# Attention with nine consecutive tokens per partition, and key-value products as row-tiled pairs of K=64

## The chip, the cores and the metric

The kernel runs on one core of one Trainium2 chip. The metric is device time in microseconds (us), the median of several executions; executions of one kernel agree within about 2%. One profiled execution per kernel gives the trace that the readings below come from; its span is about 2 us shorter than the device time. PE is TensorE's matrix unit, PEld its weight loads, DVE is VectorE, ACT is ScalarE, POOL is GpSimd, SP the engine that issues most transfers. K is the number of rows over which a matmul sums, the first number of forms such as `128*128` and `64*128` in the profile; 128 is the largest in these traces, and a matmul with K=128 is called a full-array matmul here. A warming matmul has no useful result; it is there to keep TensorE's clock up (e11, with more of them in the head than e6, ran the same last 36 K=64 matmuls of the head in 1.31 us instead of 2.10).

## The reference

Linear attention, then a two-layer network with a gated unit, in fp32:

```python
# q, k, v: [8 batches, 8 heads, 576 tokens, 64]
q_s = exp(q - max) / sum over the 64 dims;   k_s = exp(k - max) / sum over the 576 tokens
kv  = einsum('bhsd,bhse->bhde', k_s, v)      # 64x64 per head
x   = einsum('bhsd,bhde->bhse', q_s, kv)     # -> [4608 tokens, 512]
h   = x @ w_in                               # 512 -> 2048
out = (h / (1 + exp(-beta * h))) @ w_out     # 2048 -> 512
```

## The kernel before

Everything of the big products is bf16. The 4,608 tokens are cut in nine slabs of 512: slab `t` (0 to 7) holds the first 512 tokens of batch `t`, slab 8 the remaining 64 tokens of all eight batches. Each slab takes 64 matmuls of 128x128 weights and 512 columns for the first layer ("pass 1", `PS<-XT,WIN`) and 64 for the second ("pass 2", `PS<-WOUT,GT`). The attention of a later batch is woven into the slabs: `spread(steps, lo, hi)` places its small matmuls at positions lo to hi of the 128.

A main load puts 4 consecutive tokens of each head on each of 128 partitions (rows of 1024 bytes); the other 64 tokens of a batch come by "remainder" loads, rows of 256 bytes, 64 partitions per batch:

```python
def src(th, b, h0, nh):
    return bass.AP(th, (b * H + h0) * S * D, [[4 * D, 128], [S * D, nh], [1, 4 * D]])
def load_rem(name, th, buf, b, hs=(0, 1)):
    for h in hs:
        a = bass.AP(th, (b + h) * H * S * D + SM * D, [[D, SR], [S * D, H], [1, D]])
        ...dma_start(buf[64 * h:64 * h + 64, :, :], a)
# key-value product: per head pair, 4 matmuls of K=128 and one for the remainder
#   (K=128 too: the other batch's half of V is zero), 20 per batch
mm(PS[bk][:, 256*n:256*n + 129], l, r_[:, 0:129], j == 0, j == 4, ...)
def attn(b):                                   # batches 3 to 7, in slabs 2 to 6
    s = spread(kv_steps(b, (0, 1)) + kv_steps(b, (2, 3)), 8, 36)
    ... # output products at 84..108, remainder output at 104..120
```

The softmax here doesn't subtract the row's maximum and nothing guards it: scores larger than these inputs give would overflow.

## Time and profile before

| | before |
|---|---|
| device time | 295.69 us, median of 3 |
| span of the profiled run | 293.8 us |
| slab 0 starts (end of the head) | 17.11 us |
| slab 0 (with the attention of batch 1 after it) | 36.58 us |
| slabs 3 to 6 | 29.62 to 29.86 us each |
| slab 7, no attention in it | 27.63 us |

The starts of slabs are the starts of their first `PS<-XT,WIN` matmul in the timeline.

The page of the profile: busy time of each engine with its share of the span, and the number of instructions; and the chain of waits that ended last, by engine:

```profile
span 293.8 us, 3723 instructions
PE 281.1 (96%) x1470; PEld 132.5 (45%) x1499; DVE 114.3 (39%) x226; ACT 164.3 (56%) x248; POOL 43.2 (15%) x69
...
PE 75%; DMA 12%; SPq 8%; POOL 2%; issue 1%; DVE 1%; ACT 0%
```

TensorE is the bound. A piece of slab 4 in the timeline (start, length, engine, line, operation, what is written from what, number; the lengths overlap because matmuls are pipelined, so read the differences of the starts):

```profile
147.42 0.22 PE L345 MATMUL PS<-VB,EK 128*128 128x129 bf16 x1
147.48 0.38 PE L345 MATMUL PS<-XT,WIN 128*128 128x512 bf16 x1
147.69 0.22 PE L345 MATMUL PS<-VB,EK 128*128 128x129 bf16 x1
147.75 0.59 PE L345 MATMUL PS<-XT,WIN 128*128 128x512 bf16 x2
148.18 0.22 PE L345 MATMUL PS<-VB,EK 128*128 128x129 bf16 x1
```

A 512-column matmul holds the array for 0.2155 us (147.48 to 147.69, and 0.43 for two), a key-value matmul for 0.055 us (147.42 to 147.48). Its weight load is hidden: the one of the matmul at 147.42 is at 147.21 and takes 0.10 us, under the 512-column matmul before it, which holds the array from 147.20 to 147.42. Both are of the form `128*128`: weight loads and matmuls on the same rows do overlap here.

The stages in windows (window, its length, then busy time and number of PE, PEld, DVE, ACT, POOL, the clock granted to TensorE, DMA share, GB/s); the stages are the head, slabs 0, 2, 4 and 7:

```profile
0.00:17.11 17.11, 13.46 (x86) 6.06 (x88) 8.97 (x27) 10.81 (x19) 11.79 (x27) 0.90 0.98 235
17.11:53.69 36.58, 33.34 (x190) 15.42 (x193) 17.29 (x40) 21.84 (x34) 6.20 (x9) 1.00 1.15 284
84.86:115.58 30.72, 29.87 (x158) 14.20 (x160) 14.79 (x26) 18.92 (x28) 6.80 (x10) 1.00 1.03 297
145.21:175.06 29.85, 29.69 (x158) 14.28 (x160) 14.80 (x26) 18.34 (x27) 3.50 (x4) 1.00 0.26 69
234.54:262.17 27.63, 27.47 (x127) 12.51 (x128) 2.77 (x4) 11.00 (x16) 0.00 (x0) 1.00 0.09 39
```

The transfers are busy through slab 2 (last two columns) and then stop mattering. How long some of the loads take from issue to landing (KB each, median us):

```profile
QF<-in_q_dram SPq DMA_DIRECT2D x6, 1024.0 KB, 8.0
VF<-in_v_dram SPq DMA_DIRECT2D x6, 1024.0 KB, 11.8
```

And of the waits of PE, the lines of the transposed Q (`QT`), whose wait falls in slab 2, and of the normalized Q (`EQ`) in the head and slab 0 (us in total, times, longest):

```profile
PE PS L343 <- POOL EQ L308: 1.6, 3, 0.9
PE PS L343 <- DVE EQ L308: 1.2, 1, 1.2
PE PS L345 <- DMA QT<-EQ: 0.7, 1, 0.7
```

### The profile page before, as it was taken

Reading aid. Unit: us, or ns where it says so; the run is one execution under the profiler, and the core shown is the slowest. Engines: PE = TensorE matmul, PEld = TensorE weight load, DVE = VectorE, ACT = ScalarE, POOL = GpSimd, SP = SyncE. Lnnn points to the kernel's source line nnn. Section 1 sums busy time; section 2 is a strip of 40 time slices with the busy share of each in tenths; the row PEclk is TensorE's granted clock in tenths of the full one; section 3 lists DMA queues with packets and bytes.
Section 4 is the critical chain, followed back from the end, with each engine's and each line's share of the span. In section 5 each row is a group of like instructions: output and inputs, shape, how many; then the busy total and the mean of one; then the engine's idle time right before and its main releaser. Section 6 shows DMA issues by size and latency. Waiting matters only on the chain.

```text
span 293.8 us, 3723 instructions
## 1 busy us (share of the span) xinstructions
PE 281.1 (96%) x1470; PEld 132.5 (45%) x1499; DVE 114.3 (39%) x226; ACT 164.3 (56%) x248; POOL 43.2 (15%) x69
## 2 busy tenths in 40 slices
PE   6999998899999989999999999999999999999994
PEld 2444444344545434544454445444544444444441
DVE  5430686313688044704391447133913400110011
ACT  4878444879677870688068907790670077017500
POOL 6640015024605200600040000000000000000000
PEclk9799999999999999999999999999999999999999
DMA  7999999999999999904970006000810030002022
GB/s 200 286 189 249 382 315 245 336 269 347 294 302 275 354 244 318 247 0 152 315 215 20 1 1 212 4 0 0 203 31 0 2 143 0 2 36 107 0 74 71
DMA packets 58290, 47.32 MB, mean 161 GB/s; under 512 B 26000, under 2 KB 54688, under 8 KB 57248
## 3 DMA queue, kind: packets, MB, share of 16 engines
q1 hardware_dynamic: 53728, 44.45, 53.3%
q0 software_dynamic: 4224, 2.10, 5.3%
q10 hardware_dynamic: 320, 0.52, 0.5%
q8 instruction: 12, 0.20, 0.3%
q14 instruction: 6, 0.05, 0.1%
HBM read 36.71 MB, written 9.44 MB: 157 GB/s over the span
## 4 chain that ended last, share of the span: by engine, by line
PE 75%; DMA 12%; SPq 8%; POOL 2%; issue 1%; DVE 1%; ACT 0%
PE PS L345 74%; SPq L251 5%; DMA VF<-in_v_dram 3%; DMA WIN<-in_moe_w_in_dram 3%; DMA QT<-EQ 3%; SPq L258 2%; DMA WST<-in_moe_w_out_dram 2%; DMA KF<-in_k_dram 2%; POOL WIN L555 1%; DVE WOUT L542 1%; SPq L629 0%; PE PS L343 0%; ACT GT L618 0%; DVE O2S L623 0%; POOL VB L323 0%
## 5 line engine op out<-in xcount | busy, mean ns | idle before, releaser
L618 ACT ACTIVATE GT<-PS,BETA 128x512 bf16<-128x512 f32 x144 | 98.4, 687 | 89.6 <-PE PS L345 89.6
L345 PE MATMUL PS<-WOUT,GT 128*128 128x512 bf16 x561 | 131.7, 379 | 0.6
L345 PE MATMUL PS<-XT,WIN 128*128 128x512 bf16 x564 | 130.9, 379 | 1.2 <-ACT XT L417 0.7
L345 PEld LDWEIGHTS PS<-WOUT,GT 128*128 128x128 bf16 x576 | 54.5, 98 | 62.2
L345 PEld LDWEIGHTS PS<-XT,WIN 128*128 128x128 bf16 x576 | 53.5, 98 | 62.3 <-ACT XT L417 1.0
L623 DVE COPY O2S<-PS 128x512 f32<-128x512 f32 x34 | 23.3, 687 | 112.6 <-PE PS L345 112.5
L345 PE MATMUL PS<-VB,EK 128*128 128x129 bf16 (+2 forms) x160 | 25.1, 209 | 1.6 <-POOL VB L323 1.4
L323 POOL CAST VB<-VF 128x512 bf16<-128x512 f32 x28 | 18.5, 662 | 35.7 <-PE PS L345 26.0
L280 ACT ACTIVATE EQ<-QF 128x512 bf16<-128x512 f32 x32 | 18.1, 619 | 9.7 <-DMA QF<-in_q_dram 9.5
L417 DVE CAST XT<-PS 128x512 bf16<-128x512 f32 x27 | 18.5, 689 | 12.0 <-PE PS L345 12.0
L306 DVE TENSOR_REDUCE QS<-EQ 128x8 f32<-128x512 bf16 (+1 forms) x22 | 20.1, 912 | 7.5 <-ACT EQ L280 7.5
L280 ACT ACTIVATE EK<-KF 128x512 bf16<-128x512 f32 x32 | 17.9, 616 | 0.9 <-DMA KF<-in_k_dram 0.7
L345 PEld LDWEIGHTS PS<-VB,EK 128*128 128x128 bf16 x160 | 13.0, 98 | 11.2 <-POOL VB L323 2.5
L308 DVE TENSOR_TENSOR EQ<-EQ,QI 128x1024 bf16<-128x1024 bf16 (+1 forms) x14 | 15.2, 1084 | 0.5
L345 PE MATMUL PS<-QT,KVD 128*128 128x512 bf16 x32 | 12.0, 381 | 1.2 <-DMA QT<-EQ 0.7
L308 POOL TENSOR_TENSOR EQ<-EQ,QI 128x512 bf16<-128x512 bf16 x8 | 8.3, 1042 | 33.0 <-DVE QI L307 32.7
L380 DVE SCALAR_TENSOR_TENSOR KVD<-PS,RC,MASK 128x128 bf16<-128x128 f32 x32 | 11.1, 350 | 3.6 <-PE PS L345 2.5
L331 POOL CAST VR<-VRF 64x512 bf16<-64x512 f32 x8 | 6.2, 776 | 40.4 <-DMA VRF<-in_v_dram 40.0
L345 PE MATMUL PS<-WARM 128*128 128x512 bf16 x28 | 10.8, 509 | 1.3 <-DVE WARM L219 1.2
L542 DVE TENSOR_SCALAR WOUT<-WST,RB 128x512 bf16<-128x512 f32 x12 | 5.0, 480 | 14.4 <-DMA WST<-in_moe_w_out_dram 14.4
L343 PE MATMUL PS<-IDB,EQ 128*128 128x128 bf16 x48 | 6.1, 228 | 2.7 <-POOL EQ L308 1.6
L345 PE MATMUL PS<-VR,EKR 128*128 128x129 bf16 (+2 forms) x40 | 8.2, 208 | 0.1
(55 smaller groups left out, 93.1 us busy)
## 6 DMA issues: line engine op xcount, KB each, us to landing
out_dram<-O2S SPq DMA_DIRECT2D x8, 1024.0 KB, 4.5
QF<-in_q_dram SPq DMA_DIRECT2D x6, 1024.0 KB, 8.0
KF<-in_k_dram SPq DMA_DIRECT2D x6, 1024.0 KB, 9.7
VF<-in_v_dram SPq DMA_DIRECT2D x6, 1024.0 KB, 11.8
WST<-in_moe_w_out_dram SPq DMA_DIRECT2D x3, 1024.0 KB, 6.7
QF<-in_q_dram SPq DMA_DIRECT2D x8, 256.0 KB, 6.0
KF<-in_k_dram SPq DMA_DIRECT2D x8, 256.0 KB, 6.5
VF<-in_v_dram SPq DMA_DIRECT2D x8, 256.0 KB, 6.6
```

Source lines behind the costliest of these rows:

```text
L251: add(SP, lambda e, c=c: e.dma_start(dst(bufs[i], c * n, n), src(th, b, c * n, n)), w=[(name, i, hp) for hp in range(c * n // 2, (c + 1) * ...
L280: add(ACTE, lambda e, o=o, a=a: e.activation(o, a, ACT.Exp), r=[(name + "f", i, hp)], w=[("e" + name, i, hp)])
L306: add(DVE, lambda e: e.tensor_reduce(s_, a, AX.X, ALU.add), r=ks, w=[("qs", i, hp0)])
L308: add(eng, lambda e: e.tensor_tensor(a, a, vb, ALU.mult), r=ks + [("qi", i, hp0)], w=ks)
L323: add(eng, lambda e: (e.copy if eng == ACTE else e.tensor_copy)(o, a), r=[("vf", i, hp), ("vone", i)], w=[("vb", i, hp)])
L331: add(POOL, lambda e, o=o, a=a: e.tensor_copy(o, a), r=[("vrf", h), ("vrone", pi, h), ("vr0", pi, h)], w=[("vr", pi, h)])
L345: add(PE, lambda e: e.matmul(o, l, r_, start=start, stop=stop), r=r, w=w, bank=[bk])
L380: add(DVE, lambda e: e.scalar_tensor_tensor(KVD[i][:, hp, :], PS[bk][:, c:c + 128], RC[i][:, hp:hp + 1], MASK[:, :], ALU.mult, ALU.mult), ...
L417: add(eng, lambda e: (e.copy if eng == ACTE else e.tensor_copy)(XT[i][:, hp, :], PS[bk][:, :]), r=[("ps", bk)], w=[("xt", i, hp)], bank=[bk])
L542: add(DVE, lambda e, f=f: e.tensor_scalar(WOUT[:, f, :], STAGE[c][:, f % 4, :], RB[:, f:f + 1], None, ALU.mult), r=SKEY[c] + ["rb"], w=[(" ...
L618: add(ACTE, lambda e: e.activation(GT[:, f, :], PS[bk][:, :], ACT.Silu, scale=BETA[:, f:f + 1]), r=[("ps", bk), "beta"], w=[("gt", f)], ba ...
L623: add(eng, lambda e: (e.copy if eng == ACTE else e.tensor_copy)(O2S[t % 2][:, u, :], PS[bk][:, :]), r=[("ps", bk)], w=[("o2", t % 2, u)], ...
```

## The change

Its intent: put all 576 tokens of a head in one layout, 9 consecutive tokens (2304 bytes) on each of 64 partitions, heads 0 to 3 on partitions 0 to 63 and heads 4 to 7 on 64 to 127. The remainder loads, their exponentials, casts, zero fills and sums go. The two halves belong to different heads, so a key-value product contracts over 64 partitions: a pair of K=64 matmuls, one on the upper and one on the lower rows of the array, into two PSUM banks. The stores of the result are cut into two halves of 64 partitions as well (not shown).

```diff
+G = 64
+NJ = S // G                                   # 9
-        def load_main(name, th, bufs, b, split=1): ...     (128 partitions x 1024 B)
-        def load_rem(name, th, buf, b, hs=(0, 1)): ...     (64 partitions x 256 B)
+        def load_one(name, th, bufs, b, split=1):
+            for c in range(split):
+                for hh in range(2):
+                    a = bass.AP(th, (b * H + 4 * hh + c * n) * S * D,
+                                [[NJ * D, G], [S * D, n], [1, NJ * D]])
+                    o = bass.AP(bufs[i], hh * G * 4 * NJ * D + c * n * NJ * D,
+                                [[4 * NJ * D, G], [NJ * D, n], [1, NJ * D]])
+                    add(SP, lambda e, o=o, a=a: e.dma_start(o, a), ...)
...
+        def kv_mm(b, lp, j, bks, c0, c1, n0, n1, first, last, vals):
+            for hh in range(2):
+                p = slice(hh * G, hh * G + G)
+                mm(PS[bks[hh]][:, c0:c1], EK[i][p, lp, j, :], VB[i][p, lp, j, n0:n1], first, last, ...)
...
         def attn(b):
-            s = spread(kv_steps(b, (0, 1)) + kv_steps(b, (2, 3)), 8, 36)
+            s = spread(kv_steps(b), 8, 36)       # 2 x 9 pairs
...                                             (fewer warming matmuls in the head; steps of 1152 columns)
```

## The prediction

> **What bounds the kernel now.** TensorE. The page gives PE 96% busy, every other engine 56% or less; the chain of waits is 75% PE. The big matmuls (128x512, 1,152 of them) follow each other every 0.2155 us in the timeline, so 248 us of the 293.8 us span is their streaming at granted clock 1.00. From 53.7 us to the end (236 us) I count 1,024 x 0.2155 + 120 key-value matmuls x 0.055 + 24 output matmuls x 0.215 + small ones = 235 us: no idle to win. Non-streaming time is in two places: the head (first slab starts at 17.1 us) and the stretch between slabs 0 and 1 (47.0 to 53.7 us), where PE waits for the V loads and their casts.
>
> **What the change does.**
> 1. Remainder loads go (256 B rows), and Q/K/V rows become 2304 B. Packet times in the trace (18 ns per 256 B, 48 per 1024 B, 84 per 2048 B) give about 9.0 instead of 10.4 us of DMA for batch 0. After slab 1 the DMA is not on the path: worth nothing there.
> 2. Exponentials, casts, sums become fewer and larger (1152 columns; 0.63 us per 512 now, so an estimated 1.3 us). Less work for ScalarE and VectorE, off the path in steady state; in the head and before slab 1 the last cast and the coarser pipeline cost about 1 us each, eating gain 1. [...]
> 3. Per batch, 20 key-value matmuls of K=128 become 18 pairs of K=64. In the timeline of slab 4 one of the 20 costs 0.055 us, weight load hidden behind its neighbours: 1.1 us per batch. If pairs run side by side and loads stay hidden, 18 x 0.06: nothing gained, nothing lost. Run serially: +0.9 us per batch, +5 in all.
> 4. But each pair stands alone between full-array matmuls (18 steps spread over 28 slots): about 99 changes to the half-array and back in batches 2 to 7. [...] No row pair is in this trace; the nearest is the 16-row beta transpose: the matmul before it stops streaming at 12.84 us, its weight load starts only at 12.93 (not pulled ahead, nothing awaited), and the next full matmul starts at 13.10. That round trip is 0.26 us, though it is also an f32 operation. At about 0.27 us per visit instead of 0.06, 99 visits add an estimated 21 us, all on the critical path.
>
> **Prediction.** I hold step 4 slightly likelier than not. Without it: 295 to 300 us. With it: 308 to 330. My middle, 308 us, lies between; range 293 to 325. Faster by over 2%: 3%; within 2%: 40%; slower: 57%.
>
> **What would show it.** In the timeline of slabs 2 to 6, first half: gaps of 0.1 us or more in PE streaming before and after each pair, weight loads of pairs not overlapping the preceding matmul; slabs with attention several us longer than slabs 7 and 8 (27.7 us). If step 4 is wrong, a pair's two matmuls start some ns apart and the next 512-column matmul follows within 0.06 (parallel) or 0.11 us (serial). Windows of 0 to 20 and 45 to 56 us show steps 1 and 2: start of slab 0 at 16 to 19 us, of slab 1 within 2 us of before.
>
> **What would make it wrong.** [...] the head gains more from longer DMA rows than I allow; [...]

The 21 us of step 4 rest on the 0.26 us of the beta transpose. Added up from 295.69 us: about 296 us without step 4 (1.4 us won in step 1, twice about 1 us lost in step 2) and about 317 us with it. The middle of 308 us was not this sum but lies between the two.

## The result, and the profile after

The changed kernel is correct and takes 333.91 us (median of 4, 332.17 to 334.72) against 296.35 us for the kernel before in the same rounds: ratio 1.126, 95% interval 1.120 to 1.132. A ratio here is the mean time of one kernel's fast runs over that of the other's of the same rounds, so it is not quite the ratio of the medians.

Where the 36.2 us of span went, by slab:

| stage | before | after | difference |
|---|---|---|---|
| head | 17.11 | 22.38 | +5.27 |
| slab 0 | 36.58 | 39.36 | +2.78 |
| slab 1 | 31.17 | 34.27 | +3.10 |
| slab 2 | 30.72 | 40.91 | +10.19 |
| slabs 3 to 6 | 118.96 | 133.84 | +14.88 |
| slabs 7, 8 | 59.25 | 59.27 | +0.02 |

The page:

```profile
span 330.0 us, 3945 instructions
PE 306.6 (93%) x1647; PEld 132.2 (40%) x1647; DVE 115.3 (35%) x209; ACT 159.2 (48%) x203; POOL 27.5 (8%) x33
...
PE 76%; DMA 15%; DVE 3%; ACT 2%; SPq 2%; POOL 1%; issue 1%; ACTq 0%
```

PE is busy for 25 us more although the arithmetic is nearly the same (about 6 us of it may be missing records, 27 x 0.2155 us: the trace before holds 1,125 of 1,152 big matmuls). "Busy" hides the first cost. It is seen in the timeline of slab 2, matmuls and weight loads together ("issue" is idle time in which the engine waited for nothing that the profile shows):

```profile
97.82 0.10 PEld L306 LDWEIGHTS PS<-VB,EK 64*128 64x128 bf16 x2 [0.42 <-issue]
97.83 0.23 PE L306 MATMUL PS<-VB,EK 64*128 64x129 bf16 x2
...
97.99 0.11 PEld L306 LDWEIGHTS PS<-XT,WIN 128*128 128x128 bf16 x2
97.99 0.61 PE L306 MATMUL PS<-XT,WIN 128*128 128x512 bf16 x2
...
98.52 0.10 PEld L306 LDWEIGHTS PS<-VB,EK 64*128 64x128 bf16 x2 [0.42 <-issue]
98.53 0.23 PE L306 MATMUL PS<-VB,EK 64*128 64x129 bf16 x2
```

From 97.83 to 98.53 are 0.70 us: two 512-column matmuls (0.43) and one pair. A visit of a pair therefore costs 0.27 us, about 0.10 before it and 0.16 from its start to the next full matmul, where one of the 20 old matmuls cost 0.055. The pair's weights are not loaded ahead: their load begins with the pair (97.82 for the pair at 97.83), and so does that of the full matmul after it (97.99). The two matmuls of a pair mostly start 3 to 4 ns apart in the trace, so they do run side by side.

The second cost is in the stages that the transfers reach (windows as before, the same stages; the clock column misses part of the low clock in the head, where the first 512-column matmuls of both kernels come 0.43 us apart, eight warming matmuls in 3.60 us, while it gives 1.00 for the first 4 us):

```profile
0.00:22.38 22.38, 12.06 (x105) 5.93 (x105) 10.04 (x23) 9.68 (x11) 9.28 (x18) 1.00 1.02 200
22.38:61.74 39.36, 35.84 (x227) 16.45 (x225) 17.73 (x35) 20.42 (x28) 2.29 (x2) 0.91 1.08 264
96.00:136.91 40.91, 36.07 (x179) 14.40 (x178) 14.15 (x25) 18.47 (x23) 4.60 (x4) 0.92 1.06 234
170.37:203.82 33.45, 33.45 (x173) 13.81 (x172) 13.43 (x23) 17.88 (x22) 2.30 (x2) 1.00 0.42 98
270.74:298.36 27.62, 27.62 (x129) 12.52 (x128) 2.77 (x4) 11.00 (x16) 0.00 (x0) 1.00 0.16 39
```

The DMA share is as high as before, but the GB/s are lower: 200 against 235 in the head, 234 against 297 in slab 2. The loads by themselves:

```profile
QF<-in_q_dram SPq DMA_DIRECT2D x12, 576.0 KB, 16.0
VF<-in_v_dram SPq DMA_DIRECT2D x12, 576.0 KB, 18.8
```

The two longest waits of PE:

```profile
PE PS L304 <- DVE EQ L284: 9.3, 3, 5.1
PE PS L306 <- DMA QT<-EQ: 4.8, 1, 4.8
```

And slab 2 in the timeline, at that wait for the transpose:

```profile
124.34 0.61 PE L306 MATMUL PS<-QT,KVD 128*128 128x512 bf16 x1 [4.84 <-DMA QT<-EQ]
124.74 2.77 PE L306 MATMUL PS<-WOUT,GT 128*128 128x512 bf16 x6
```

A transfer of about half the bytes takes up to twice as long to land: 16.0 us against 8.0 for Q, 18.8 against 11.8 for V (each also queues behind the others: 576 KB alone would take an estimated 2.6 us at the 225 GB/s given below). Most of the 9.3 us are waits for the normalized Q (`EQ`) of batches 0 and 1 (5.07 and 3.49 us), against 2.8 us for `EQ` in all before; only a part of them comes from the transfers, as 6.7 us will be left in e5, where the loads are fast. The transpose of Q goes through the same queue (SP) behind the loads, 5.4 us from issue to landing in the median and 16.2 at most; PE waits 4.84 us for it, and afterwards the 512-column matmuls come 0.43 us apart ((2.77 - 0.63) / 5) instead of 0.2155. The clock granted is 0.50 from 124.30 to 128.00 us and 1.00 again from 130.00 to 136.00; slab 2 of the kernel before, where PE waited 0.7 us for the transpose, has 1.00 in the mean. So the wait also cost clock.

The packet records of the two traces give the time of one packet by its length (worked out from all packets of the trace):

| packet | before, median ns | after, median ns |
|---|---|---|
| 1024 B (main loads before) | 48 | - |
| 2304 B (all loads after) | - | 168 |
| 2048 B | 84 | 84 |

From before's 1024 and 2048 byte packets I had interpolated 94 ns for 2304 bytes. With 16 engines, 2304 B / 168 ns is 219 GB/s; by the bytes landed, the loads of batch 0 moved at 225 GB/s (2.27 to 17.98 us). The first packets, the 189 that start before 4.0 us, have a median of 93 ns here too; those of batch 0 after them, 169 ns. The 84 ns for 2048 B after mixes two kinds of transfer: in the last four halved stores the packets of this length have a median of 153 ns.

### The profile page after: what moved, and what is told of

It is laid out like the page before. It is cut to its first block, busy times and chain, and to the rows that moved or that the text cites. A ratio compares the mean times of both kernels' runs of the same rounds, so it can differ in the third digit from the quotient of the medians.

```text
span 330.0 us, 3945 instructions
## 1 busy us (share of the span) xinstructions
PE 306.6 (93%) x1647; PEld 132.2 (40%) x1647; DVE 115.3 (35%) x209; ACT 159.2 (48%) x203; POOL 27.5 (8%) x33
## 4 chain that ended last, share of the span: by engine, by line
PE 76%; DMA 15%; DVE 3%; ACT 2%; SPq 2%; POOL 1%; issue 1%; ACTq 0%
PE PS L306 75%; DMA QT<-EQ 5%; DMA QF<-in_q_dram 3%; DMA WIN<-in_moe_w_in_dram 3%; DMA KF<-in_k_dram 2%; DMA WST<-in_moe_w_out_dram 2%; SPq L240 2%; POOL WIN L497 1%; PE PS L304 1%; DVE EQ L284 1%; DVE QS L275 1%; ACT L257 1%; ACT EQ L257 1%; DVE WOUT L481 1%; DVE O2S L313 0%
## 5 line engine op out<-in xcount | busy, mean ns | idle before, releaser
L306 PE MATMUL PS<-XT,WIN 128*128 128x512 bf16 x576 | 142.5, 381 | 0.2 <-ACT XT L313 0.2
L306 PE MATMUL PS<-VB,EK 64*128 64x129 bf16 (+2 forms) x360 | 28.4, 221 | 3.9 <-ACT EK L257 2.4
L313 DVE CAST XT<-PS 128x512 bf16<-128x512 f32 (+1 forms) x35 | 21.9, 630 | 24.8 <-PE PS L306 24.8
L306 PEld LDWEIGHTS PS<-VB,EK 64*128 64x128 bf16 x360 | 13.7, 98 | 40.0 <-issue 34.0
L290 POOL CAST VB<-VF 128x1152 bf16<-128x1152 f32 x14 | 16.1, 1150 | 136.7 <-DMA VF<-in_v_dram 108.7
L275 DVE TENSOR_REDUCE QS<-EQ 128x18 f32<-128x1152 bf16 x16 | 21.6, 1347 | 14.5 <-ACT EQ L257 14.4
L306 PE MATMUL PS<-QT,KVD 128*128 128x512 bf16 (+1 forms) x64 | 18.9, 310 | 4.9 <-DMA QT<-EQ 4.8
L257 ACT ACTIVATE EK<-KF 128x1152 bf16<-128x1152 f32 x16 | 17.9, 1152 | 6.1 <-DMA KF<-in_k_dram 6.1
L257 ACT ACTIVATE EQ<-QF 128x1152 bf16<-128x1152 f32 x16 | 17.9, 1156 | 5.3 <-DMA QF<-in_q_dram 5.2
L284 DVE TENSOR_TENSOR EQ<-EQ,QI 128x1152 bf16<-128x1152 bf16 (+1 forms) x15 | 19.8, 1322 | 0.5
L366 DVE SCALAR_TENSOR_TENSOR KVD<-PS,RC,MASK 128x128 bf16<-128x128 f32 x32 | 10.8, 349 | 1.9 <-PE PS L306 0.9
## 6 DMA issues: line engine op xcount, KB each, us to landing
VF<-in_v_dram SPq DMA_DIRECT2D x12, 576.0 KB, 18.8
```

The source lines that it names most:

```text
L257: add(ACTE, lambda e: e.activation(o, half(srcb[i], lp), ACT.Exp), r=[(name + "f", i, hh, lp) for hh in range(2)], w=[("e" + name, i, lp, ...
L275: add(DVE, lambda e: e.tensor_reduce(s_, a, AX.X, ALU.add), r=[("eq", i, lp, j) for j in range(NJ)], w=[("qs", i, lp)])
L284: add(eng, lambda e: e.tensor_tensor(a, a, vb, ALU.mult), r=ks + [("qi", i, lp)], w=ks)
L290: add(eng, lambda e: (e.copy if eng == ACTE else e.tensor_copy)(o, half(VF[i], lp, j0, n)), r=[("vf", i, hh, lp) for hh in range(2)] + [(" ...
L306: add(PE, lambda e: e.matmul(o, l, r_, start=start, stop=stop), r=r, w=w, bank=[bk])
L313: add(eng, lambda e: (e.copy if eng == ACTE else e.tensor_copy)(o, a), r=r, w=w, bank=[bk])
```

## The experiments

Two theories, each for a part of the loss. **S (switching)**: each visit of a K=64 pair between full-array matmuls costs 0.27 us, laid to switching the array there and back; about 100 visits (the trace has 100 in slabs 1 to 6), some 21 us. **H (half the partitions)**: a load to 64 partitions moves at about half the rate of one to 128 (168 ns a packet where I had reckoned with 94); it delays the head, slab 0 and slab 2 by the other 15 us. Rivals: K=64 matmuls are slow in themselves (K); the long rows are slow (L); the coarse steps of 1152 columns hold up the head (G).

### e1_group: the pairs in one block

```diff
-            s = spread(kv_steps(b), 8, 36)
+            s = spread(kv_steps(b), 7, 8)
-            ... spread(kv_steps(b), 95, 104)     (batch 2)
+            ... spread(kv_steps(b), 103, 104)
```

> The changed kernel, with the 18 key-value pairs of a batch issued as one block (slot 8) instead of spread over 28 slots; nothing else. Theory S (switching): each visit of a pair costs 0.108 us before it and 0.16 us from its start to the next full-array matmul, 0.27 us in all, because the array is switched; in a block the switch is paid once. Then slabs 3 to 6 fall from 33.46 us to about 29.8 us, 18 pairs take about 1.2 us together, and the total falls by about 20 us, to about 313 us. Rival K (a K=64 pair is slow by itself, its weights never hidden): pairs still take 0.2 us or more each in the block, slabs stay at 33 us, total within 3 us of 334.

Measured: correct, 317.04 us, ratio to before 1.073. Slabs 3 to 6 take 30.08 us instead of 33.46. The block in the timeline (the first pair went one slot ahead, so there are two visits):

```profile
136.69 0.39 PE L306 MATMUL PS<-XT,WIN 128*128 128x512 bf16 x1
137.01 1.17 PE L306 MATMUL PS<-VB,EK 64*128 64x129 bf16 x34
138.34 2.97 PE L306 MATMUL PS<-XT,WIN 128*128 128x512 bf16 x13 [0.16 <-issue]
```

Thirty-four matmuls, 17 pairs, take about 0.95 us ((1.17 - 0.22) for their starts), 0.056 us a pair, so rival K falls: inside the block a pair is as cheap as one old matmul. Its weight loads (99 ns in the mean) overlap there with the pairs before: the idle time before them in which the engine waited for nothing falls from 34.0 us in the changed kernel to 4.3. The total fell by 17 us, not by 20: PE now reached the transpose in slab 2 earlier and waited 9.6 us for it instead of 4.8. The gain was partly handed to the other bottleneck:

```profile
PE PS L306 <- DMA QT<-EQ: 9.6, 1, 9.6
```

### e8_before_visit64 and e9_before_visit128: the switch by itself, on the kernel before

```diff
+        def visit():                             # 18 per slab in slabs 2 to 6, at slots 44 to 72
+            bk = bank()
+            mm(PS[bk][:, 0:128], WARM[0:64, 0:128], WARM[0:64, 0:128], True, True, ...)   # e9: 0:128
-            return s
+            return s + spread([lambda: visit() for _ in range(18)], 44, 72)
```

> The kernel before, with 18 extra lone matmuls per slab in slabs 2 to 6 (zeros, 128 columns, K=64 on partitions 0 to 63, result unused) between full-array matmuls. Theory S: each costs about 0.27 us of PE time (0.11 before it, 0.16 to the next start), so slabs 3 to 6 grow by about 4.8 us each and the total by about 24 us, to 319 to 321 us. Rival (the cost lies in pairs on two halves or in waits for data): each costs its 0.055 us, total within 6 us of before.

> The control of the K=64 visits: the kernel before with the same 18 extra lone matmuls per slab, but with K=128 (zeros, 128 columns). Theory S: no switch, so each costs about 0.055 us, slabs 3 to 6 grow by 1.0 us and the total by about 5 us, to 300 to 302 us. If extra matmuls cost as much whatever their K, it is near 318 us like the K=64 run.

Measured: both correct. K=64: 318.22 us, ratio 1.073, just under the expected range; slab 3 takes 34.40 us against 29.62, 0.266 us a visit. K=128: 300.02 us, ratio 1.020 (interval 1.012 to 1.028); slab 3 takes 30.63 us, 0.056 us a visit. First K=64, then K=128:

```profile
130.58 0.61 PE L345 MATMUL PS<-XT,WIN 128*128 128x512 bf16 x2
131.12 0.23 PE L345 MATMUL PS<-WARM 64*128 64x128 bf16 x1
131.28 0.60 PE L345 MATMUL PS<-XT,WIN 128*128 128x512 bf16 x2
```

```profile
126.14 0.22 PE L345 MATMUL PS<-WARM 128*128 128x128 bf16 x1
126.19 0.59 PE L345 MATMUL PS<-XT,WIN 128*128 128x512 bf16 x2
126.62 0.22 PE L345 MATMUL PS<-WARM 128*128 128x128 bf16 x1
```

The only difference is the number of rows. A lone K=64 matmul, without a partner, without new data to wait for, with zeros for operands, costs what a pair costs. S is shown as a cost of changing between K=128 and K=64, and its size. The number of visits confirms it: slabs 3 to 6 take 33.46 us with 18 visits, 30.08 with 2 (e1) and 29.87 with 1 (e10, below), 0.21 us for each visit removed, which is 0.27 less 0.056. What the array does at a change is not shown; the 0.21 us are about two weight loads (93 to 98 ns each), and the traces say only that these are not loaded ahead there.

### e2_dma and e3_group_dma: one transfer per head pair over 128 partitions

```diff
-                for hh in range(2):
-                    a = bass.AP(th, (b * H + 4 * hh + c * n) * S * D, [[NJ * D, G], [S * D, n], [1, NJ * D]])
+            for l in range(4):
+                a = bass.AP(th, (b * H + l) * S * D, [[4 * S * D, 2], [NJ * D, G], [1, NJ * D]])
+                o = bass.AP(bufs[i], l * NJ * D, [[4 * NJ * D, 2 * G], [1, NJ * D]])
```

(e3 adds the edit of e1.)

> The changed kernel, with each load of Q, K, V issued as one transfer per head pair (h, h+4) over all 128 partitions instead of two heads over 64 partitions: the same 2304-byte rows, the same bytes, the same number of loads in the head. Theory H (half the partitions): packets of 2304 bytes fall from 168 ns median to 90 to 115 ns, slab 0 starts at 17.5 to 19.5 us instead of 22.4, the 4.8 us wait for QT in slab 2 is gone, total falls by 10 to 15 us, to 319 to 324 us. Rival L (the long rows of 2304 bytes are slow): packets stay near 168 ns and the total stays within 2 us of 334. Rival G (the coarser steps of 1152 columns, not the transfers, hold up the head): packets get faster but slab 0 still starts after 20.5 us.

> Both of the above edits together. If S and H hold and are independent, the two gains add: 298 to 303 us, slabs 3 to 6 at about 29.8 us, slab 0 starting at 17.5 to 19.5 us. If either is wrong its share stays: about 313 (only S right) or 321 (only H right).

Measured: both correct, 738.59 us (ratio 2.50) and 731.51 us (ratio 2.47). None of the theories had this. The throughput of e2 in 40 slices of its 736 us span:

```profile
GB/s 43 51 78 112 187 105 52 51 52 52 51 51 102 52 51 52 52 52 51 51 52 51 52 108 65 52 51 96 78 51 52 81 74 90 2 89 22 37 57 58
```

It sits at 52 GB/s for most of that time, while its 2304-byte packets take 93 ns: two packets in flight at a time would move 2 x 2304 B / 93 ns = 50 GB/s, and the page puts the busy share of the 16 DMA engines at one tenth in these slices, so they did about the work of two. The loads of e5 (below) also reach 128 partitions in rows of 2304 bytes and move at 349 GB/s; what differs is the address pattern, whose first dimension in the source is 2 here and 128 there, and the size of a transfer, 288 KB here and 576 or 1152 there. Why most of the engines' time goes unused here is not shown. The experiment was badly made for its purpose, but says one thing: a row of 2304 bytes is not slow, 93 ns where I had estimated 94. Rival L falls (e5 has the 93 ns and slices of 380 to 398 GB/s in which the 16 engines are at least 90% busy).

### e4_before_half: the loads of the kernel before, by halves

```diff
-                add(SP, lambda e, c=c: e.dma_start(dst(bufs[i], c * n, n), src(th, b, c * n, n)), ...)
+                for hh in range(2):
+                    a = bass.AP(th, (b * H + c * n) * S * D + hh * 64 * 4 * D,
+                                [[4 * D, 64], [S * D, n], [1, 4 * D]])
+                    o = bass.AP(bufs[i], hh * 64 * H * 4 * D + c * n * 4 * D,
+                                [[H * 4 * D, 64], [4 * D, n], [1, 4 * D]])
+                    add(SP, lambda e, o=o, a=a: e.dma_start(o, a), ...)
```

> The kernel before, with each main load of Q, K, V cut into two transfers of 64 partitions each; rows stay 1024 bytes. Theory H: packets of 1024 bytes rise from 48 ns median to 70 ns or more, slab 0 starts 2 to 5 us later, total rises by 4 to 15 us, to 300 to 311 us. Rival L: packets stay at about 48 ns and the total rises by less than 1.5 us (only the extra issues).

Measured: correct, 322.75 us, ratio 1.091. Packets of 1024 bytes rise from 48 to 78 ns median. Slab 0 starts at 27.91 us, and in slab 2 PE has the same wait as in the changed kernel, only longer:

```profile
PE PS L350 <- DMA QT<-EQ: 10.7, 1, 10.7
PE PS L350 <- ACT VB L328: 6.4, 3, 3.5
```

Slabs 3 to 6 are unchanged (29.62 to 29.86 us). The direction is H's, with rows of 1024 bytes; the size is above my range. This kernel also issues twice as many main loads and still has the remainder loads, and the trace shows that this, and not the packets, is most of what delays its head: the eight issues of V of batch 0 take from 13.25 to 18.43 us and end 9.3 us later than before (9.12).

```profile
13.25 5.18 SPq L256 DMA_DIRECT2D VF<-in_v_dram  x8
```

The 1024-byte packets of batch 0 still take 46 ns (median of the 2,687 of 3,072 that start before 20 us; 46 in the kernel before too), with 14 packets in flight on average. From slab 0 to the end of slab 2 they take 80 ns against 49, with about 18 in flight in both kernels. So of the 26.8 us by which the span grew, 10.8 in the head belong mostly to the issues and 17.2 in slab 2 to the transfers (slab 0 takes 1.2 less); only slab 2 speaks for H.

### e5_evenodd and e6_group_evenodd: 128 partitions, 16 engines, wrong result

If the upper half takes the even heads and the lower half the odd ones, the step from partition to partition is uniform and one transfer reaches all 128. The features then meet the wrong rows of the first weight matrix; the work is the same.

```diff
-                for hh in range(2):
-                    a = bass.AP(th, (b * H + 4 * hh + c * n) * S * D,
-                                [[NJ * D, G], [S * D, n], [1, NJ * D]])
+                a = bass.AP(th, (b * H + 2 * c * n) * S * D,
+                            [[NJ * D, 2 * G], [2 * S * D, n], [1, NJ * D]])
```

(e6 adds the edit of e1.)

> Wrong result on purpose. The changed kernel, but the upper 64 partitions take the even heads and the lower 64 the odd ones, so that the address step from partition to partition is uniform and one transfer covers 128 partitions on all 16 engines; rows of 2304 bytes and total bytes as in the changed kernel (features end up at the wrong rows of the first weight matrix). Theory H [...]: packets of 2304 bytes 90 to 115 ns median instead of 168, slab 0 starts at 17.5 to 19.5 us instead of 22.4, no 4.8 us wait for QT in slab 2, total 317 to 324 us. Rival G (coarse steps of 1152 columns hold up the head whatever the transfers do): packets fast, but slab 0 starts after 20.5 us.

> Wrong result on purpose, as the even/odd run, plus the 18 pairs of a batch as one block. S and H together are the whole loss: 296 to 303 us, slabs 3 to 6 at 30.1 us as in the grouped run. If a third cost is hidden, over 305 us.

Measured: wrong results. e5: 314.34 us, ratio 1.060. e6: 296.24 us, ratio 0.999 (0.994 to 1.004). Packets of 2304 bytes fall from 168 to 93 ns in both; 16 x 2304 B / 93 ns is 396 GB/s, and the fastest slices of e5 have 380 to 398; by the bytes landed, the loads of batch 0 move at 349 GB/s in e5 (225 in the changed kernel). That e5 issues half as many transfers is not the cause: the changed kernel had 16.8 packets in flight on average during these loads, so its engines did not wait for issues. In e5 slab 0 starts at 15.68 us, 1.4 us earlier than in the kernel before and 6.7 us earlier than in the changed one, so rival G falls as the cause of the late head. Time and start lie below what I expected of e5: the gain is larger. The waits of PE in e5, whole: the wait for the transpose is gone, 6.7 of the 9.3 us for `EQ` are not, so the coarser steps may still cost something.

```profile
PE PS L304 <- DVE EQ L284: 6.7, 3, 3.5
PE PS L306 <- DVE WARM L215: 1.2, 1, 1.2
PE PS L306 <- ACT XT L313: 0.2, 1, 0.2
```

e5 mends the transfers alone and gains 19.6 us by the medians, e1 mends the switching alone and gains 16.9, e6 both and gains 37.7 (the kernel before stood at 295.5 to 296.6 us in all these rounds). In the total, the two causes are the whole loss. By slab, e6 is not the kernel before: its head and slab 0 are 2.0 us shorter, slab 1 is 1.8 us longer and slabs 3 to 6 together 1.4 us (two visits are left). The causes are not quite independent: the switching hid some of the wait for the transpose, as e1 shows.

### e7_group_actq: the halves from two queues

```diff
-                    add(SP, lambda e, o=o, a=a: e.dma_start(o, a), ...)
+                    add(ACTE if hh else SP, lambda e, o=o, a=a: e.dma_start(o, a), ...)     # and e1's edit
```

> Correct result. The grouped kernel with the loads of the lower 64 partitions issued from the ScalarE queue, those of the upper 64 from the SyncE queue, so that both halves are filled at the same time. Theory H: packets of 2304 bytes fall to 95 to 130 ns, total 298 to 308 us (ScalarE also has to issue, some 0.5 us each). If the cost were one per transfer of 64 partitions and not of the half being alone, packets stay near 168 ns and the total near 317 us.

Measured: correct, 306.21 us, ratio 1.031, in the expected range; against e1's 1.073 the two queues win 4%. (An issue by ScalarE took 0.50 us in the trace before, median of 4 stores: the 0.5 us of the expectation.) The profiled run: slow (311.29 us), so its stages are not compared; its 2304-byte packets took 114 to 116 ns on the two queues against 168 in the changed kernel, and the loads of batch 0 moved at 272 GB/s against 228 in e1. So transfers of 64 partitions each lose less when both halves are filled at once; that it is the halves and not the second queue, no run separates.

### e10_fixed and e11_fixed_warm: a correct kernel with both causes removed

```diff
+        # loads as in e5; the 18 pairs in one visit:  spread(kv_steps(b), 7.5, 8)
-                copy(eng, XT[i][:, hp, :], PS[bk][:, :], ...)
+                for a in range(2):                    # each half to the rows that WIN expects
+                    m, p, f = 2 * (hp % 2) + a, G * (hp // 2), G * a
+                    copy(eng, XT[i][p:p + G, m, :], PS[bk][f:f + G, :], ...)
+        # e11 only: warm(24) for warm(8), warm(3) for warm(1), second V cast of batch 1 on ScalarE
```

> Correct result. The changed kernel with even heads above and odd heads below (one load over 128 partitions), the pairs of a batch as one block in one visit, and the output copies cut by halves so that each half lands at the rows where the first weight matrix expects it (8 copies of 64 partitions per batch instead of 4 of 128). Slabs 3 to 6 about 29.8 us; slab 0 starts about 1 us later than the 16.3 us of the grouped even/odd run because of the extra copies; total 295 to 300 us, within 2% of before.

> Correct result. The same, with 24 warming matmuls instead of 8 at the start and 3 instead of 1 between the later steps of the head, and the second V cast of batch 1 on ScalarE. The 36 pairs of the head took 2.1 us in the grouped even/odd run against 1.2 us in slab 0, which is a low clock; warming should bring slab 0 forward by 0.5 to 1 us, and the cast should bring slab 1 forward by about 1 us: total 1 to 2 us less than the run without, 294 to 298 us.

Measured: both correct, 298.15 us (ratio 1.010) and 297.96 us (ratio 1.010). Slabs 3 to 6 take 29.87 us. Slab 0 starts at 16.83 and 16.81 us. The warming worked on what it aimed at (the last 36 K=64 matmuls of the head, 18 pairs, which the expectation calls 36 pairs, took 1.31 us instead of the 2.10 of e6) and the total did not follow: the time before slab 0 had moved to the doubled copies, which take 0.58 to 0.69 us for 64 partitions just as they did for 128. The gain of 1 to 2 us that I expected of e11 is not there.

No version beats the kernel before: with both faults mended, the new layout is level with it or 1% behind.

## Why the prediction was wrong

- **Step 1 failed, and it is the step that put the result out of range.** It read "Packet times in the trace (18 ns per 256 B, 48 per 1024 B, 84 per 2048 B) give about 9.0 instead of 10.4 us of DMA for batch 0. After slab 1 the DMA is not on the path: worth nothing there." I costed a packet by its length alone. The length was right, 93 ns in e5 against my 94; but the change also cut each load to 64 partitions, and then it took 168 ns after the first few, so the loads of batch 0 took 15.7 us (1536 packets; 10.1 us in e5, where they reach 128 partitions; 12.3 before) instead of 9. In place of a gain of 1.4 us stand the later head (+5.3), part of slab 0, and a wait in slab 2 that I had declared off the path: 4.84 us and the low clock (0.50) after it. e5 prices the step at 19.6 us; slab 2 of e4 shows it on the other kernel. Why 64 partitions are slower is not shown; the runs give the size, 219 GB/s by the packet times and 225 by bytes landed. I did not ask about it, because the diff looked like a change of rows and not of partitions.
- **Step 4 was right in size and in where the cost falls.** "About 0.27 us per visit instead of 0.06, 99 visits add an estimated 21 us, all on the critical path": measured 0.27 us in the changed kernel and 0.266 us for a lone K=64 matmul (e8), against 0.055 and 0.056 for K=128; slabs 3 to 6 grew by 3.7 us each. The one small-row matmul that the old trace contained, the beta transpose with its 0.26 us, had shown it. These runs show the cost at the change, not what the array does there.
- **Step 3 was right**: pairs side by side, 0.056 us a pair inside a block (e1).
- **Step 2 is in part open.** It expected about 1 us lost in the head and 1 before slab 1. The coarser steps did not make the head longer than before (e5: slab 0 at 15.68 us), but in e5 the loads of batch 0 end 2.2 us earlier than before and slab 0 starts only 1.4 us earlier, so a loss of that size in the head is not refuted. Fewer warming matmuls did cost clock, 2.10 us for the last 18 pairs in e6 against 1.31 in e11, but that was not what slab 0 waited for in e11.
- **The form of the estimate.** "My middle, 308 us, lies between" two branches, 295 to 300 and 308 to 330, and neither contained the transfers. With step 4 and nothing else the sum is about 317 us (296.35 + 21), and e5, which has only the switching, measured 314.34; the missing 17 to 20 us are the mis-sized transfers.
- What stays open: what the array does at a change of K; why a load to 64 partitions moves at 225 GB/s and e2's at 52; and why slab 1 is longer than before in e6.

## What to carry to other kernels

Count the visits, not the matmuls: a row-tiled pair (two K=64 matmuls on separate rows) is as cheap as a full matmul inside a block (0.056 us) and five times as dear between full-array matmuls (0.27 us), so in a mixed stream like this one batch the matmuls of one K. When a change alters the shape of a load, ask which partitions each single transfer reaches and how its address pattern is cut, before asking how long its rows are; here the same rows of 2304 bytes moved at 52 GB/s (e2: 128 partitions, the source's first dimension 2), 225 (the change: 64 partitions) and 349 (e5: 128 partitions, first dimension 128), the last two by bytes landed. And a transfer that was off the path here did not stay off it when the transfers lost their rate (a wait of 0.7 us for the transpose became 4.84): look at what is queued behind them.
